# End units of both batches first, keys stored by batch, values of a phase in six shared tiles: a fused attention and gated projection kernel

## The chip, the cores and the metric

The kernel runs on one core of a Trainium2 chip. The metric is the device time of one execution in microseconds, lower is better.

## The reference

Block-sparse attention for 4 batches, 8 heads, 768 positions in 24 blocks of 32, head size 64. A query block attends to its own block and its two neighbours, to the first and the last block, and to three blocks drawn for it at run time; the first and the last query block attend to everything. Then a gated layer: a causal convolution of width 5 over the positions gives a gate, and the gated value projection is projected again.

```python
scores = scale * np.matmul(q, k.transpose(0, 1, 3, 2))
mask = np.abs(blk_i - blk_j) <= window
mask = mask | (blk_i == 0) | (blk_j == 0) | (blk_i == n_blocks - 1) | (blk_j == n_blocks - 1)
for qb in range(n_blocks):
    for kb in sampled_blocks[qb]:
        mask[qb * block:(qb + 1) * block, kb * block:(kb + 1) * block] = True
attn = softmax(np.where(mask, scores, -1e9))
x = np.matmul(attn, v)                      # heads side by side: (4, 768, 512)
gate_pre = sum over k of conv_w[k] * xp[:, k:k + S, :]
return (1.0 / (1.0 + np.exp(-gate_pre)) * (x @ w_val)) @ w_out
```

## The kernel before

Two phases of two batches each (`F`, `E`). The work of a phase is a list of parts: 22 pair parts (one inner query block i for both batches) and two end parts (query blocks 0 and 23 of one batch), which `GLOB_AT` puts at places 7 and 13 of phase 0. A pair part is one unit, an end part two, so there are 52 units.

A unit goes through four stages in successive steps of the main loop: `scores` (matmuls into PSUM, maximum on VectorE, exponential on ScalarE), `transposes` one step later (TensorE, evicted by ScalarE), `values` two steps later, `finish` three steps later (VectorE writes the rows, transposed, into `xT`). A pair unit scores 8 blocks held side by side in a ring of key tiles `kg`, filled by `copy_keys`: GpSimd copies blocks out of the tile `keys`, which holds all keys of the phase, by block and then by batch, and from block 19 on SP loads the drawn blocks from memory. Its values come as two operands: `va` (first and last block in the upper half, the pair's own two blocks in the lower, loaded by SP) and `vb` (neighbour and three drawn blocks, gathered by an indirect DMA on GpSimd with indices `idx`). An end unit scores against all 24 blocks in `keys` and takes its values from `vn`, one tile per batch in one buffer.

Three more jobs run beside the units. `decode_weights` turns 64-bit weights into two 32-bit parts on VectorE, `gates` and `split` prepare 384 rows of one batch for the layer on VectorE and ScalarE, `project` does its matmuls on TensorE. There are eight such row groups; the first needs all weights decoded and 12 query blocks finished. How many calls of them stand in each step is written out by hand in two strings of digits, two per step: `FILLS` (calls of `project`, 11 per row group) and `STEPS` (calls of decode, four per weight, or of a gate, 20 each; each group of them also advances a split). `WEIGHTS_AT`, `K_AT`, `KEY_PARTS` and `V_AT` say at which step or part a load is issued; all on SP's queue, in program order. Every engine's program order is fixed. At the start, 17 matmuls on a tile of ones keep TensorE busy (`WARM`), and VectorE computes the validity of the drawn blocks and the gather indices before the first unit.

Of the kernel before, what the change touches and what calls it, by code (L numbers as in the profile page):

```python
# [39 lines left out]
WARM = 17  # L40
# [5 lines left out]
    "41531212300155012103532311"  # L46
    "01035112303331022123021212"
    "00101201115004112130012510"
    "10100011122154101010100113"
    "4130"  # L50
)
STEPS = (
    "15212121013020010424122120"
    "21003221303420341233043241"
    "11132111152345310421322323"
    "14511004324143101000444354"
    "5525"
# [5 lines left out]
def attention_moe(ctx, tc, qb, kb, v, ve, sampled, w_val, conv_w, w_out, ident_in, slot_in, out):  # L63
# [11 lines left out]
    class InOrder:  # L75
# [23 lines left out]
    sp.dma_start(  # L99
        sb.rearrange("p i r w -> p (i r w)"),  # L100
        bass.AP(tensor=src.tensor, offset=src.offset, ap=[[0, 128], [1, NB * NR * 2]]),
    )
# [12 lines left out]
    act.activation(warm, warm, AF.Exp)  # L115
    sm = const.tile([1, NB * NR], I32, name="sm")
    dve.tensor_copy(sm, sb[0:1, :, :, 0].rearrange("p i r -> p (i r)"))
    sf = const.tile([128, NR, NB], F32, name="sf")
    dve.tensor_copy(sf, sb[:, :, :, 0].rearrange("p i r -> p r i"))

    base = const.tile([128, NB], F32, name="base")
    valid = const.tile([128, NB], F32, name="valid")
    off = slot[:, 2 * NB : 2 * NB + 1]
    dve.tensor_scalar(out=base[0:32, :], in0=slot[0:32, 0:NB], scalar1=off[0:32], scalar2=None, op0=ALU.add)
    dve.memset(valid, 1.0)
    dve.memset(valid[0:32, 1:2], 0.0)
    dve.memset(valid[0:32, NB - 2 : NB - 1], 0.0)
    vm = const.tile([128, NR, NB], F32, name="vm")  # L130
    tmp = const.tile([128, NR, NB], F32, name="tmp")
    dve.tensor_scalar(out=vm, in0=sf, scalar1=0.0, scalar2=None, op0=ALU.not_equal)
    dve.tensor_scalar(out=tmp, in0=sf, scalar1=float(NB - 1), scalar2=None, op0=ALU.not_equal)
    dve.tensor_tensor(out=vm, in0=vm, in1=tmp, op=ALU.mult)
    for r in range(NR):
        dve.tensor_tensor(out=tmp[:, r, :], in0=sf[:, r, :], in1=slot[:, NB : 2 * NB], op=ALU.subtract)
    dve.tensor_tensor(out=tmp, in0=tmp, in1=tmp, op=ALU.mult)
    dve.tensor_scalar(out=tmp, in0=tmp, scalar1=1.5, scalar2=None, op0=ALU.is_gt)
    dve.tensor_tensor(out=vm, in0=vm, in1=tmp, op=ALU.mult)
    for r in range(1, NR):  # L140
        for e in range(r):
            dve.tensor_tensor(out=tmp[:, 0, :], in0=sf[:, r, :], in1=sf[:, e, :], op=ALU.not_equal)
            dve.tensor_tensor(out=vm[:, r, :], in0=vm[:, r, :], in1=tmp[:, 0, :], op=ALU.mult)
    for r in range(NR):
        rows = slice(32 * (r + 1), 32 * (r + 2))
        dve.tensor_copy(valid[rows, :], vm[rows, r, :])
        dve.tensor_scalar(
            out=base[rows, :], in0=sf[rows, r, :], scalar1=float(BLK), scalar2=off[rows], op0=ALU.mult, op1=ALU.add
        )
    idx = const.tile([128, F, NB], I32, name="idx")  # L150
    def indices(f):

        row = const.tile([128, NB], F32, tag=f"row{f}", name="row")
        dve.tensor_scalar_add(row, base, float(f * S - F * S))
# [11 lines left out]
    waiting, copies, holding = [], [], [False]  # L166
# [84 lines left out]
    for f in range(F):  # L251
        ph = Phase()
        ph.f = f
        ph.xT, ph.vn = {}, {}
        ph.done, ph.queued, ph.read = set(), set(), [set() for _ in range(NT)]
        phases.append(ph)

    phase_of = [-1] * NB

    def load_all_keys():  # L260
        for f in range(F):
            for a, z in KEY_PARTS[f]:
                sp.dma_start(keys[:, a:z], kb[:, f, a:z])
                phase_of[a:z] = [f] * (z - a)
                yield

    def load_phase_values(ph):
        for e in range(E):
            vn = ph.vn[e] = const.tile([128, S // 128, H * DV], F32, tag="vn", name="vn")
            for c in range(3):  # L270
                r0 = ph.f * S + 256 * c
                sp.dma_start(
                    vn[:, 2 * c : 2 * c + 2, :],
                    v[r0 : r0 + 256, e * H * DV : (e + 1) * H * DV].rearrange("(c p) d -> p c d", p=128),
                )
# [9 lines left out]
    for ph in phases:  # L285
# [3 lines left out]
        for place, i in enumerate(order):  # L289
# [4 lines left out]
            if not pr.glob:  # L294
                pr.j, pr.p = (i - 1) % 2, (i - 1) // 2
                pr.kg = kg[pr.seq // 2 % 2]
# [6 lines left out]
    def block_numbers(pr, eng):  # L303
# [9 lines left out]
        for n, reg in zip(mine, regs):  # L313
            yield 1 + n, reg

    def one(block):
        return block.rearrange("p o e x -> p (o e x)")
# [5 lines left out]
    def load_keys(pr):  # L323
# [3 lines left out]
        if f and pr.i == 2:  # L327
            sp.dma_start(pr.kg[:, 0, 0:2], kb[:, f, 0 : NB : NB - 1])
        if not pr.glob:
            for place, reg in block_numbers(pr, SP):  # L330
                sp.dma_start(one(pr.kg[:, 1 + pr.j, place : place + 1]), one(kb[:, f, bass.ds(reg, 1)]))
# [546 lines left out]
```

## Time and profile before

| | us |
|---|---|
| median of 3 runs | 358.65 |
| lowest and highest | 357.97, 362.62 |
| the profiled execution's own time | 356.5 |
| its span, first to last instruction | 354.7 |
| TensorE busy in the span | 330.0 |
| VectorE busy | 273.8 |
| ScalarE busy | 229.5 |
| GpSimd busy | 96.6 |

The span is counted from the first instruction of the program; what lies around it is the difference to the time. Shares of busy time are means over stretches that have different limits, and TensorE's busy time is modelled, so the rows below are of stretches and of single instructions.

### The profile page before, as it was taken

The page shows a single profiled execution, that of the slowest core. Times are in us where ns is not written, and L with a number is a line of the kernel's source. Part 1 is how long each engine was busy: PE and PEld are TensorE (multiplying, and loading weights), DVE is VectorE, ACT ScalarE, POOL GpSimd, SP SyncE. Part 2 cuts the span into 40 slices and gives each one's busy share as a digit, 9 for nine tenths or more (in the row PEclk, how much of TensorE's full clock was granted, in tenths as well). Part 3 has the DMA queues.
Part 4 walks back from the last instruction along what each step waited for, and adds up shares of the span by engine and source line. Part 5 has one row for each costly group of instructions (what it writes and reads, how often), then busy time and mean ns, then how long its engine had stood idle before and what let it go on. Part 6 is the DMA issues. An engine that isn't in the chain of part 4 may idle for free.

```text
span 354.7 us, 15350 instructions
## 1 busy us (share of the span) xinstructions
PE 330.0 (93%) x6530; PEld 260.0 (73%) x6530; DVE 273.8 (77%) x665; ACT 229.5 (65%) x512; POOL 96.6 (27%) x146
## 2 busy tenths in 40 slices
PE   8589878887988999999999999999999999999995
PEld 7256656665655887797778777887778877988894
DVE  4277759978999899658988995659986489989640
ACT  2396657987888667656676674767667495565421
POOL 0776346536432032414331122221132010000000
PEclk9969989999999999999999999999999999999999
DMA  7998868876489997997698476636896022010202
GB/s 260 343 321 244 264 226 268 270 226 203 117 261 277 386 295 249 300 297 225 216 269 266 130 253 206 198 99 213 242 277 200 5 63 91 2 68 23 89 0 89
DMA packets 36707, 71.20 MB, mean 201 GB/s; under 512 B 4320, under 2 KB 21216, under 8 KB 36256
## 3 DMA queue, kind: packets, MB, share of 16 engines
q1 hardware_dynamic: 29728, 46.56, 41.5%
q0 software_dynamic: 6336, 23.43, 21.0%
q8 instruction: 51, 0.84, 1.0%
q10 hardware_dynamic: 576, 0.24, 0.2%
q14 instruction: 16, 0.13, 0.1%
HBM read 63.92 MB, written 6.29 MB: 198 GB/s over the span
## 4 chain that ended last, share of the span: by engine, by line
PE 59%; DVE 25%; ACT 8%; issue 3%; DMA 3%; SPq 0%; POOLq 0%; POOL 0%; ACTq 0%; DVEq 0%
PE op L81 13%; PE vp L81 12%; PE av L81 11%; PE pt L81 10%; PE sc L81 9%; DVE th L81 9%; DVE mx L81 6%; ACT pe L81 3%; DMA k<-in_k 3%; PE s L81 3%; ACT ptr L81 2%; DVE xl L81 2%; ACT th L81 2%; DVE wst L81 1%; DVE y L81 1%
## 5 line engine op out<-in xcount | busy, mean ns | idle before, releaser
L81 ACT ACTIVATE pe<-sc,mx 128x256 f32<-128x256 f32 x176 | 69.4, 478 | 42.1 <-DVE mx L81 42.0
L81 POOL DMA_INDIRECT vb<-in_v,idx x44 | 45.5, 1034 | 176.4 <-PE av L81 152.8
L81 DVE SCALAR_TENSOR_TENSOR th<-xT,cw,th 128x384 f32<-128x384 f32 x128 | 76.6, 625 | 4.6 <-ACT th L81 4.6
L81 DVE TENSOR_REDUCE mx<-sc 128x2 f32<-128x512 f32 x88 | 56.4, 681 | 30.7 <-PE sc L81 30.7
L81 ACT COPY ptr<-pt 128x512 f32<-128x512 f32 x112 | 63.7, 607 | 13.2 <-PE pt L81 11.6
L81 PE MATMUL sc<-kg,qc 64*32 64x256 f32 x1408 | 53.9, 393 | 9.1 <-ACT pe L81 3.3
L81 POOL COPY kg<-k 128x256 f32 (+1 forms) x97 | 50.6, 560 | 11.7 <-PE sc L81 10.8
L81 PE MATMUL op<-wo,yh 128*128 128x512 f32 x192 | 52.9, 397 | 0.1
L81 PE MATMUL pt<-ident,pe 128*128 128x128 f32 x352 | 52.5, 285 | 0.1
L81 PE MATMUL vp<-xh,wv 128*128 128x384 f32 x256 | 51.4, 342 | 0.0
L81 PEld LDWEIGHTS pt<-ident,pe 128*128 128x128 f32 x352 | 39.8, 143 | 6.8 <-issue 0.8
L81 PEld LDWEIGHTS vp<-xh,wv 128*128 128x128 f32 x256 | 44.1, 188 | 0.6 <-DVE y L81 0.4
L81 PEld LDWEIGHTS sc<-kg,qc 64*32 64x32 f32 x1408 | 22.9, 108 | 28.7 <-issue 12.8
L81 PEld LDWEIGHTS av<-va,ptr 128*32 128x32 f32 x1408 | 23.2, 110 | 25.3 <-ACT ptr L81 12.0
L81 PEld LDWEIGHTS op<-wo,yh 128*128 128x128 f32 x192 | 35.1, 188 | 7.2 <-ACT yh L81 0.5
L81 PE MATMUL av<-va,ptr 128*32 128x65 f32 x1408 | 32.3, 224 | 4.4 <-ACT ptr L81 2.0
L81 ACT CAST yh<-y 128x384 fp32r<-128x384 f32 x32 | 16.8, 524 | 22.8 <-DVE y L81 22.8
L81 PE MATMUL op<-wo,yl 128*128 128x512 f32 x96 | 30.8, 402 | 0.0
L81 PE MATMUL av<-vb,ptr 128*32 128x65 f32 x1408 | 28.9, 220 | 1.9 <-issue 1.9
L81 PE MATMUL vp<-xl,wv 128*128 128x384 f32 x128 | 27.4, 334 | 0.0
L81 DVE TENSOR_TENSOR yl<-y,yh 128x384 fp32r<-128x384 f32 x32 | 18.2, 568 | 10.4 <-ACT yh L81 10.1
L81 PEld LDWEIGHTS av<-vb,ptr 128*32 128x32 f32 x1408 | 23.8, 110 | 2.2 <-issue 2.0
(73 smaller groups left out, 389.6 us busy)
## 6 DMA issues: line engine op xcount, KB each, us to landing
kg<-in_k SPq DMA_DIRECT2D x78, 128.0 KB, 5.0
vn<-in_v SPq DMA_DIRECT2D x12, 520.0 KB, 6.3
qc<-in_q SPq DMA_DIRECT2D x48, 128.0 KB, 4.6
out<-ot SPq DMA_DIRECT2D x23, 256.0 KB, 2.4
va<-in_v SPq DMA_DIRECT2D x22, 260.0 KB, 5.9
k<-in_k SPq DMA_DIRECT2D x3, 1024.0 KB, 8.3
k<-in_k SPq DMA_DIRECT2D x6, 512.0 KB, 7.0
wst<-in_w_val SPq DMA_DIRECT2D x4, 512.0 KB, 8.4
```

Of the source, the lines that this page charges most:

```text
L81: made = getattr(self.eng, name)(*args, **kwargs)
```

## The change

The end parts of phase 0 go to places 0 and 0, so units 0 to 3 are end units, batch 0 first. `keys` is laid out by batch and then by block, and loaded per batch in thirds, batch 0 ahead of everything but the first query tile; the block numbers come behind it. End units score in four groups of matmuls (blocks 0 and 23; 1 to 6; 7 to 14; 15 to 22) in place of three. The values of a phase lie in six tiles of 128 rows for both batches, in memory with block 23 next to block 0, so that `ve` is no longer an input; in phase 0 a pair's `va` is one of these tiles or a tile filled by GpSimd copies of 64 rows, and in phase 1 every second pair's rows still come by a DMA. Validity and base rows move from VectorE to GpSimd, and the indices are computed in step 3. Of an end unit's three evictions in phase 0 the middle one moves from ScalarE to VectorE. Load places, warming matmuls and both strings of digits are other ones.

```diff
-GLOB_AT = ((7, 13), (12, 18))
-V_AT = ((6, 8, 10, 13, 13, 14), (0, 5, 12, 20, 23, 23))
-KEY_PARTS = (((16, 24), (0, 8), (8, 16)), ((0, 4), (4, 8), (8, 12), (12, 16), (16, 20), (20, 24)))
-K_AT = (0, 0, 0, 22, 23, 24, 24, 25, 25)
+GLOB_AT = ((0, 0), (12, 18))
+V_AT = ((0, 0, 1, 1, 1, 1, 2, 2, 3, 4, 4, 5), (0, 0, 3, 12, 12, 16))
+KEY_PARTS = (((0, 0, 8), (0, 8, 16), (0, 16, 24), (1, 0, 8), (1, 8, 16), (1, 16, 24)), tuple((E, a, a + 4) for a in range(0, NB, 4)))
+K_AT = (0, 0, 0, 1, 1, 1, 22, 24, 24, 24, 27, 29)
-WEIGHTS_AT = (0, 2, 6, 7, 8, 10, 15, 19)
+WEIGHTS_AT = (2, 6, 8, 9, 11, 12, 14, 19)
-WARM = 17
+VALUES_FROM = 4
+INDEX_AT = 3
+WARM = 13
+EVICTED = (4,)
 FILLS = (
+    "03551521524012114220200213"
+    "11120302053001132011022121"
+    "03100402104453112111312511"
+    "10100001111545201000000101"
+    "2154"
 STEPS = (
+    "35440005001114434131202031"
+    "01301003113322311155014114"
+    "55402320303154220043344354"
+    "23450102032554452123143312"
+    "4525"
...
+    def validity():
+        pool.tensor_scalar(out=base[NR * BLK :, :], in0=slot[NR * BLK :, 0:NB], scalar1=off[NR * BLK :], scalar2=None, op0=ALU.add)
+        pool.memset(valid, 1.0)
...
+        pool.tensor_scalar(out=vm, in0=sf, scalar1=0.0, scalar2=None, op0=ALU.is_gt)
+        pool.tensor_scalar(out=tmp, in0=sf, scalar1=float(NB - 1), scalar2=None, op0=ALU.is_lt)
+        pool.tensor_tensor(out=vm, in0=vm, in1=tmp, op=ALU.mult)
...
-    keys = const.tile([128, NB, E, HP * BLK], F32, name="k")
+    keys = const.tile([128, E, NB, HP * BLK], F32, name="k")
...
-        for e in range(E):
-            vn = ph.vn[e] = const.tile([128, S // 128, H * DV], F32, tag="vn", name="vn")
...
+        for e in range(E if ph.f == 0 else 1):
+            for c in range(S // 128):
+                if e == 0:
+                    ph.vn.append(const.tile([128, E, H * DV], F32, tag=f"vn{c}", name="vn"))
+                r0 = ph.f * S + 128 * c
+                some = slice(e, e + 1) if ph.f == 0 else slice(0, E)
+                sp.dma_start(ph.vn[c][:, some], v[r0 : r0 + 128, :].rearrange("p (e d) -> p e d", e=E)[:, some])
...
+        if pr is parts[0]:
+            load_numbers()
...
-            if first:
-                act.copy(kt[:, 0, 0:2], keys[:, 0 : NB : NB - 1])
-            (act.copy if first else pool.tensor_copy)(kt[:, 0, 2:4], keys[:, i0 : i0 + 2])
-            pool.tensor_copy(kt[:, 1:3, 0], keys[:, i0 - 1 : i0 + 3 : 3])
+            if pr.ph.f == 0 and i0 == 1:
+                pool.tensor_copy(kt[:, 0, 0:2], blocks(0, NB, NB - 1))
+            pool.tensor_copy(kt[:, 0, 2:4], blocks(i0, i0 + 2))
+            pool.tensor_copy(kt[:, 1:3, NR], blocks(i0 - 1, i0 + 3, 3))
...
-            if pr.p < 2 - (f == 0):
-                sp.dma_start(vt[0 : 2 * BLK].rearrange("p e d -> p (e d)"), ve[f])
-            sp.dma_start(vt[64:128].rearrange("p e d -> p (e d)"), v[r0 : r0 + 2 * BLK, :])
+            c, r0 = divmod(2 * BLK * (pr.p + 1), 128)
+            pr.va = va[pr.p % 2] if r0 == 0 or f else ph.vn[c]
+            ends = [] if pr.p == 0 or f == 0 and r0 == 0 and pr.p > 1 or f and pr.p > 2 else [ph.vn[0][0 : 2 * BLK]]
+            own = [ph.vn[c][0 : 2 * BLK]] if r0 == 0 else []
...
+            def copy_rows():
+                for rows in ends:
+                    pool.tensor_copy(pr.va[0 : 2 * BLK], rows)
+                for rows in own:
+                    pool.tensor_copy(pr.va[2 * BLK :], rows)
+            owns.append(copy_rows)
...
-            for k0 in range(3):
+            for dst, a, z, by in ((lo, 0, NB, NB - 1), (lo, 1, 7, 1), (lo, 7, 15, 1), (hi, 15, NB - 1, 1)):
...
-            act.copy(t, pt)
+            (dve.tensor_copy if un.pr.glob and un.pr.ph.f == 0 and len(un.PT) in EVICTED else act.copy)(t, pt)
...
-            indices(0)
-            more_keys()
-            more_values()
-            more_values()
-            until("copied", 1, copy_keys)
+            while more_keys():
+                pass
+            block_copies()
+            validity()
+        elif n < VALUES_FROM:
+            until("copied", 5, copy_keys)
+            while more_keys():
+                pass
...
+            if n == INDEX_AT:
+                indices(0)
...
+                run(owns)
...
-    nc = bacc.Bacc("TRN2", target_bir_lowering=False, num_devices=1)
+    nc = bacc.Bacc("TRN2", target_bir_lowering=False, num_devices=1, dynamic_dma_scratch_size=4096)
```

## Rows read from the trace of the kernel before

**Rows 1.** Chain of work that ended last: start, us, what.

```profile
2.61 10.49 DMA k<-in_k
14.38 1.20 PE sc L81 x32
...
115.80 4.17 PE vp L81 x24
...
342.51 8.25 PE op L81 x36
```

**Rows 2.** The same chain, single stages of units, without a wait inside.

```profile
28.31 1.05 PE av L81 x64
29.36 1.02 PE pt L81 x8
30.39 1.02 PE sc L81 x32
...
219.24 1.46 PE s L81 x48
...
226.37 1.50 PE av L81 x96
```

**Rows 3.** Busy time by stretch; columns: length, PE, PEld, DVE, ACT, POOL, clock, DMA.

```profile
15.56:56.80 41.24, 34.99 (x937) 23.46 (x938) 29.71 (x74) 29.71 (x68) 24.63 (x42) 0.88 0.86 272
56.80:110.90 54.10, 46.68 (x1396) 32.63 (x1393) 49.68 (x119) 44.45 (x104) 24.36 (x43) 1.00 0.74 226
115.60:297.00 181.40, 180.77 (x3711) 145.91 (x3710) 146.46 (x357) 123.68 (x277) 40.58 (x47) 1.00 0.70 217
297.00:354.70 57.70, 53.14 (x325) 46.99 (x323) 38.50 (x78) 24.87 (x51) 0.00 (x0) 1.00 0.12 46
```

**Rows 4.** Timeline of the head: warming matmuls, first key copies and what they waited for.

```profile
1.11 10.02 PE L81 MATMUL idle<-ones 128*128 128x256 f32 x34 [1.11 <-POOL ones L81]
10.41 1.14 ACT L81 COPY kg<-k 128x512 f32<-128x512 f32 x2 [4.79 <-DMA k<-in_k]
```

**Rows 5.** Timeline, VectorE: reductions of unit 0, of both end units, of the next.

```profile
15.56 1.29 DVE L81 TENSOR_REDUCE mx<-sc 128x2 f32<-128x512 f32 x2 [6.15 <-PE sc L81]
...
43.19 1.02 DVE L81 TENSOR_REDUCE mx<-s 128x1 f32<-128x512 f32 x2 [0.93 <-PE s L81]
...
50.26 1.02 DVE L81 TENSOR_REDUCE mx<-s 128x1 f32<-128x512 f32 x2 [2.54 <-PE s L81]
...
56.80 1.24 DVE L81 TENSOR_REDUCE mx<-sc 128x2 f32<-128x512 f32 x2
```

**Rows 6.** Groups by shape: count, busy us, mean ns of one, idle time before.

```profile
L81 DVE SCALAR_TENSOR_TENSOR th<-xT,cw,th 128x384 f32<-128x384 f32 x128 | 76.6, 625 | 4.6 <-ACT th L81 4.6
L81 DVE TENSOR_REDUCE mx<-sc 128x2 f32<-128x512 f32 x88 | 56.4, 681 | 30.7 <-PE sc L81 30.7
L81 POOL DMA_INDIRECT vb<-in_v,idx x44 | 45.5, 1034 | 176.4 <-PE av L81 152.8 <-DVE idx L81 8.6 <-issue 8.3
L81 POOL COPY kg<-k 128x256 f32 x54 | 21.8, 441 | 0.7 <-DMA k<-in_k 0.6
L81 DVE TENSOR_TENSOR x<-av,rs 128x256 f32<-128x256 f32 x48 | 19.9, 414 | 0.4
L81 DVE STREAM_TRANSPOSE xT<-x 128x256 f32<-128x256 f32 x44 | 18.9, 431 | 0.0
L81 DVE RECIPROCAL rs<-rs 128x4 f32<-128x4 f32 x48 | 7.7, 160 | 0.1
L81 DVE SCALAR_TENSOR_TENSOR wst<-wst 128x512 int32<-128x512 int32 x8 | 6.6, 827 | 0.1
```

**Rows 7.** Timeline: one decode instruction with and without GpSimd copies beside it.

```profile
25.45 1.39 DVE L81 SCALAR_TENSOR_TENSOR wst<-wst 128x512 int32<-128x512 int32 x1
25.53 1.55 POOL L81 COPY kg<-k 128x256 f32 x3
...
38.18 0.70 DVE L81 SCALAR_TENSOR_TENSOR wst<-wst 128x512 int32<-128x512 int32 x1
```

More of the change, by code (lines that the diff above doesn't have):

```diff
@@ L62, in attention_moe @@
 @with_exitstack
-def attention_moe(ctx, tc, qb, kb, v, ve, sampled, w_val, conv_w, w_out, ident_in, slot_in, out):
+def attention_moe(ctx, tc, qb, kb, v, sampled, w_val, conv_w, w_out, ident_in, slot_in, out):
     nc = tc.nc
@@ L137, in attention_moe @@
[L137 to L148, printed above, removed]
-        )
@@ L164, in attention_moe @@
     cw = const.tile([128, CH, KW], F32, name="cw")
-    waiting, copies, holding = [], [], [False]
+    waiting, copies, owns, holding = [], [], [], [False]
     def behind(*calls):
@@ L295, in attention_moe @@
                 pr.j, pr.p = (i - 1) % 2, (i - 1) // 2
+                pr.first = [x for x in parts if not x.glob][-1] if pr.j else pr
                 pr.kg = kg[pr.seq // 2 % 2]
@@ L313, in block_numbers @@
         for n, reg in zip(mine, regs):
-            yield 1 + n, reg
-    def one(block):
-        return block.rearrange("p o e x -> p (o e x)")
+            yield n, reg
     def load_queries(pr):
@@ L327, in load_keys @@
         if f and pr.i == 2:
-            sp.dma_start(pr.kg[:, 0, 0:2], kb[:, f, 0 : NB : NB - 1])
+            for n in range(2):
+                sp.dma_start(pr.kg[:, 0, n], kb[:, f, :, n * (NB - 1)])
         if not pr.glob:
             for place, reg in block_numbers(pr, SP):
-                sp.dma_start(one(pr.kg[:, 1 + pr.j, place : place + 1]), one(kb[:, f, bass.ds(reg, 1)]))
+                sp.dma_start(pr.kg[:, 1 + pr.j, place], kb[:, f, :, bass.ds(reg, 1)].rearrange("p e o x -> p e (o x)"))
         for _ in range(K_AT.count(parts.index(pr))):
             next(loading_keys)
+        if pr is parts[0]:
+            load_numbers()
         if pr is not parts[-1]:
@@ L337, in load_keys, with blocks @@
             next(loading_values[f])
+    def blocks(a, z, by=1):
+        return keys[:, :, a:z:by].rearrange("p e n x -> p n e x")
     def copy_keys(pr):
@@ L343, in copy_keys @@
         numbers = {eng: list(block_numbers(pr, eng)) for eng in (POOL, ACT)}
-        assert set(phase_of[i0 - 1 : i0 + 3] if pr.j == 0 else ()) <= {pr.ph.f}
-        assert not any(numbers.values()) or set(phase_of) == {pr.ph.f}
+        mine = {(f, e) for f in range(pr.ph.f + 1) for e in range(E)}
+        assert all(x == mine for x in (phase_of[i0 - 1 : i0 + 3] if pr.j == 0 else ()))
+        assert not any(numbers.values()) or all(x == mine for x in phase_of)
         if pr.j == 0:
-            first = pr.ph.f == 0 and i0 == 1
-            if first:
-                act.copy(kt[:, 0, 0:2], keys[:, 0 : NB : NB - 1])
-            (act.copy if first else pool.tensor_copy)(kt[:, 0, 2:4], keys[:, i0 : i0 + 2])
-            pool.tensor_copy(kt[:, 1:3, 0], keys[:, i0 - 1 : i0 + 3 : 3])
+            if pr.ph.f == 0 and i0 == 1:
+                pool.tensor_copy(kt[:, 0, 0:2], blocks(0, NB, NB - 1))
+            pool.tensor_copy(kt[:, 0, 2:4], blocks(i0, i0 + 2))
+            pool.tensor_copy(kt[:, 1:3, NR], blocks(i0 - 1, i0 + 3, 3))
         for place, reg in numbers[POOL]:
-            pool.tensor_copy(one(kt[:, 1 + pr.j, place : place + 1]), one(keys[:, bass.ds(reg, 1)]))
+            pool.tensor_copy(kt[:, 1 + pr.j, place], keys[:, :, bass.ds(reg, 1)].rearrange("p e o x -> p e (o x)"))
         def rest():
             for place, reg in numbers[ACT]:
-                act.copy(one(kt[:, 1 + pr.j, place : place + 1]), one(keys[:, bass.ds(reg, 1)]))
+                act.copy(kt[:, 1 + pr.j, place], keys[:, :, bass.ds(reg, 1)].rearrange("p e o x -> p e (o x)"))
             if pr.i == 3:
```

114 lines of the change are left out of this document (57 added, 57 removed).

## The prediction

> **What bounds the kernel now.** I read the chain of work that ended last first, then the busy time by stretch, then the instructions of the stretches that the chain points to. The chain begins with a DMA of keys that ends at 13.10 us, the first scores follow at 14.38, and from 115.80, the first matmul of a projection, to 350.76, the last, it is nearly all TensorE [rows 1]. So the kernel has three parts: a head without work for TensorE, a stretch with units alone, and from 115.80 a stretch in which projections fill every gap.
>
> That the last stretch is TensorE's own can be worked out without its busy share, which is modelled. A pair unit costs it 1.02 (scores) + 1.02 (transposes) + 1.05 (values) = 3.09 us, an end unit 1.46 + 1.5 x 1.02 + 1.50 = 4.49 [rows 2], a projection 2 x 4.17 + 8.25 = 16.59 [rows 1]. 44 pair units, 8 end units and 8 projections make 136.0 + 35.9 + 132.7 = 304.6 us. By 115.80 the scores of units 0 to 22, the values of 0 to 20 and the transposes of 0 to 20 and half of 21 are done: 73.1 us. The other 231.5 are done in the 238.9 us that are left, 3.9 of which come after the last matmul. TensorE's lost time is therefore nearly all ahead of 115.80: 42.7 us, of which 14.4 are the head and 28.3 lie between units.
>
> What makes the units slow there is VectorE. From the first reduction to that of unit 9 it is busy 29.71 of 41.24 us, from there to the reduction of unit 21 49.68 of 54.10, while TensorE has 3.09 us of work in a step of some 4.1 [rows 3]. It decodes the weights and makes the first gates in these steps. Later it has slack (146.46 of 181.40) and TensorE has none [rows 3].
>
> The time therefore follows from one number: when the first projection starts, and how many units are done by then. From the digits of STEPS, 36 decode calls, 20 calls for a gate and 6 for a split, I count that the first projection starts in step 22 before and in step 23 after. So after the change one more pair unit is done when it starts, and end = start + 238.9 - 3.1.
>
> **The change part by part.**
> *Head.* Before, the first scores need copies from two of three 1 MB pieces, and the second 1 MB has landed at 10.41 [rows 4], the third at 13.10 [rows 1]: 2.7 us per MB. After, unit 0 reads the keys of one batch straight from their tile, three pieces of 0.5 MB, with one query tile ahead. Counted back from 10.41 by half a MB, they land at about 9.0. The warming matmuls took 10.02 us for 34 records from 1.11 on [rows 4]; 13 in place of 17 of them end at about 8.8. Bounds for the first scores: 8.8 and 10.4; I take 9.0, so the first reduction is at 10.2 (before 15.56): 5.4 us earlier.
>
> *Four end units in a row.* A step between two end units can't be shorter than TensorE's 4.49. Before, the reductions of the two end units and of the unit behind them stand at 43.19, 50.26 and 56.80: steps of 7.1 and 6.5 us, with four decode calls in the second [rows 5]; after, steps 2 and 3 have no decode call. Bounds 4.5 and 6.8. I take 4.8, nearer to the lower end since VectorE has 2 x (1.02 + 0.16) of reductions and one eviction of 0.7 in such a step (its length from the reduction of as many elements, 0.681 [rows 6]) and waits for the rest of it. Unit 4 is reduced at 10.2 + 19.2 = 29.4; then two pair steps with an end unit's values or transposes in them (3.95 + 0.4) and three of 3.95, the mean from 15.56 to 43.19, seven steps [rows 5]: unit 9 at 49.9, against 56.80.
>
> *VectorE from unit 9 to the projection.* To the reduction of unit 21 it had 49.68 us. After, to that of unit 22: one more pair unit (2 x 0.681 + 0.414 + 0.431 + two small ones of 0.16 = +2.5); both end units have left this stretch (-2.0 in reductions); decode calls 22 in place of 16, at most 0.827 each (+5.0); gate calls 12 in place of 21, some 8 multiply-adds of 0.625 fewer (-5.0) [rows 6]. Sum +0.5. The four evictions moved to VectorE lie in the end steps, where it waits, and cost nothing; without that cover 2.8 us. Validity leaves VectorE at a time when it was idle: worth nothing.
>
> *GpSimd beside VectorE.* GpSimd gets some 7 copies of 64 x 1040 values in this stretch, in place of DMAs. No row has one: by elements it is four times the 256-element copy, at most 4 x 0.441 = 1.8 us [rows 6]; I take 1.3. A VectorE instruction of 0.70 us took 1.39 while three GpSimd copies ran for 1.55 [rows 7], so at most 0.45 us is lost per us of copying: 0 to 4.1, I take 2.0. [...] With the old idle time of 4.4 the stretch takes 49.7 + 0.5 + 2.0 + 4.4 = 56.6 us. Unit 22 is reduced at 106.5; the projection starts 4.9 later, as before (110.90 to 115.80): 111.4. Bounds for the idle time: 0, and 8.8 as twice the old.
>
> *Behind the start.* Gate calls that were done by then are owed later, 5.0 us of VectorE. Its slack of 35 us in that stretch [rows 3] hides that if it falls in the right steps; bounds 0 and 5, I take 1.0. End units have 32 score matmuls in place of 24 for the same 768 columns. 16 of their records are 64 columns wide; at the 0.0164 us that a 65-column record costs (1.05 / 64) [rows 2] that is 0.14 us a unit, 0.6 for the four units of the second phase. Bounds 0 and 2.
>
> *Hidden parts.* Validity on GpSimd is 27 instructions of at most 0.441 us each: up to 12 us from about 10, when the block numbers (now behind the keys on SP's queue) have landed. Behind them on GpSimd wait the key copies for unit 4, 4 us, ready by 26 at the latest, needed at 28. That cover is thin at its upper end; each us over it would be paid once. The index computation sits in step 3 on VectorE, and the first gather follows in step 4; its rows are needed at step 6, 8 us later. SP issues some 20 loads at the start; the first batch's values are behind 5.0 MB, at 2.7 us per MB about 18, and are needed in step 2, about 20. The removed value DMAs were late for nobody. On SP the reload of the first value tile waits for GpSimd's last copy out of it, and the second phase's key loads are queued behind; they are needed some three steps later.
>
> **The sum.** 111.4 + 238.9 - 3.1 + 1.0 + 0.6 = 348.8 us of span, 5.9 under 354.7. The profiled execution took 356.5 us, 1.8 more than its span, and the median of the runs is 358.65. Taking the saving from the median: 352.7. A measurement here can tell about 2%, 7.2 us, from no change.
>
> **The rivals.**
> *More than that.* If the end steps take 4.5 us and the idle 4.4 us of the second stretch vanish, because steps with pair units alone are more even, the start is at 105.8 and the time 347.1. For it: VectorE's load per step is evener. Against: decode calls crowd into steps 8 to 17.
> *The early start is lost again.* Weights arrive later (first decode of a weight in step 5, not 2), and 6 decode calls are moved into the stretch where VectorE is already 92% busy. If unit 22 comes no earlier than unit 21 did, only 3.1 - 1.6 are left: 357.1. The change would then have moved the wait from the keys to VectorE.
> *GpSimd becomes the bound, and it is slower than before.* For two units it makes two gathers of 1.034, six copies of 256 elements and two of 512 [rows 6]. At the 0.52 us a piece of 256 that it took beside VectorE [rows 7] this is 2.1 + 5.2, and a row copy of four pieces adds 2.1: 9.4 us, where two steps are 8.2. From unit 4 to 19 that is 0.6 us a unit, 9.6 in all: 362.3. At 0.44 it comes to 8.2 and just fits, so a contended copy decides. Against it: the copies for a unit are asked for two steps ahead, and the first nine units before, seven of them pairs, kept GpSimd busy for only about 60% of the time (24.63 of 41.24) [rows 3].
>
> **How the numbers follow.** Forecast 0.41 (352.7, its own range 348 to 357), more 0.26, lost again 0.19, GpSimd 0.14. Faster by over 2% (under 351.5) is the second case and a third of the forecast: 0.39. Slower by over 2% (over 365.8) is a third of the last: 0.05. The range leaves out half of the last case and the far end of the second: 345.5 to 361.
>
> **What would show it.** First scores near 9.0 and no idle TensorE before them; reductions of the end units 4.5 to 5.5 us apart; first projection matmul near 111 with the scores of unit 23 done; VectorE over 90% busy in the 50 us before; from there TensorE as full as before. Wrong if the first projection starts after 114, if key copies on GpSimd release scores again and again, or if VectorE's two-input instructions are longer throughout.

## The result and the profile after

The changed kernel takes 360.12 us (median of 20 runs, 356.69 to 362.65), the kernel before 358.78 in the same comparison (20 runs); the ratio is 1.0056 with a 95% interval of 1.0031 to 1.0081. The forecast was 352.7 and faster; 360.12 lies near the upper end of the whole range given, 345.5 to 361. Medians here are over all runs of a comparison and ratios over undisturbed runs alone, so the two can differ by a few tenths of a per cent. The profiled execution took 360.51 us with a span of 358.7 (before 356.5 and 354.7).

Busy time by stretch, kernel after, columns as in [rows 3]: first reduction to unit 9, unit 9 to the end of unit 22's reduction, the projections, the tail.

```profile
10.67:53.70 43.03, 36.19 (x1126) 26.46 (x1111) 30.14 (x78) 28.75 (x65) 30.69 (x65) 0.96 0.71 246
53.70:116.70 63.00, 49.62 (x1358) 34.95 (x1356) 60.02 (x127) 45.11 (x108) 46.44 (x66) 0.92 0.69 219
120.50:299.00 178.50, 176.01 (x3660) 142.30 (x3659) 147.43 (x352) 122.46 (x273) 47.72 (x54) 1.00 0.63 193
299.00:358.70 59.70, 56.10 (x337) 49.82 (x335) 40.04 (x81) 25.68 (x51) 0.00 (x0) 0.99 0.14 53
```

The first row shows what the head gave: 10.67 where [rows 5] had 15.56. The second shows where it went: VectorE (third pair of numbers) is busy 60.02 of 63.00 us, and GpSimd's 46.44 us are nearly twice the 24.36 of [rows 3]. TensorE's granted clock, 1.00 there before, is 0.92.

The chain of work that ended last, kernel after (start, us, what): the whole of it, then its pieces between 100 and 125 us.

```profile
1.10 8.45 PE idle L84 x26
13.16 2.91 PE s L84 x61
...
80.92 3.16 DVE wo L84
...
100.68 1.93 DVE th L84
...
120.96 3.39 DVE th L84 x2
...
346.74 8.38 PE op L84 x36
```

Before the projections it runs over VectorE, and the pieces that stick out are single decode and gate instructions of two to three us, where [rows 6] has 0.6 to 0.8. Their surroundings, timeline of the kernel after (start, us, engine, line, operation, tiles, count, and in brackets the idle time before and what ended it):

```profile
61.42 0.96 POOL L84 DMA_INDIRECT vb<-in_v,idx  x1 [0.52 <-PE av L84]
61.49 0.67 DVE L84 SCALAR_TENSOR_TENSOR wst<-wst 128x512 int32<-128x512 int32 x1
62.19 2.90 DVE L84 SCALAR_TENSOR_TENSOR words<-words,wst 128x512 int32<-128x512 int32 x1
62.38 1.06 POOL L84 COPY vn<-vn 64x1040 f32<-64x1040 f32 x1
63.38 2.65 POOL L84 COPY kg<-k 128x512 f32<-128x512 f32 x5
65.57 0.67 PE L84 MATMUL av<-va,ptr 128*32 128x65 f32 x32 [2.41 <-DVE x L84]
...
80.38 0.96 POOL L84 DMA_INDIRECT vb<-in_v,idx  x1 [1.28 <-PE av L84]
80.85 3.24 DVE L84 TENSOR_TENSOR wo<-words,wo 128x512 fp32r<-128x512 f32 x1
81.34 1.06 POOL L84 COPY vn<-vn 64x1040 f32<-64x1040 f32 x1
82.34 2.69 POOL L84 COPY kg<-k 128x512 f32<-128x512 f32 x5
84.89 1.09 PE L84 MATMUL av<-va,ptr 128*32 128x65 f32 x32 [2.77 <-DVE x L84]
86.79 1.78 PE L84 MATMUL pt<-ident,pe 128*128 128x128 f32 x8
90.58 1.09 PE L84 MATMUL pt<-ident,pe 128*128 128x128 f32 x8
```

The row copy (64 x 1040, new in this kernel) stands directly behind a gather and ahead of five key copies, so GpSimd copies for 3.7 us without a gap, and no gap lies between the gather and the first copy either. A VectorE instruction of 0.7 us that falls into that run lasts 2.9 or 3.2; both of these began while the gather still ran. Behind it on VectorE waits the small multiply that frees the values' PSUM tile, and TensorE idles 2.4 and 2.8 us for it (`<-DVE x`). After the second of these idle times the eight transposes take 1.78 us instead of 1.09. Busy time by short stretches there, the clock is the third number from the end:

```profile
74.00:78.00 4.00, 3.67 (x80) 3.20 (x88) 3.23 (x9) 2.48 (x7) 2.97 (x7) 0.57 0.18 58
84.80:88.50 3.70, 3.60 (x72) 3.29 (x73) 2.73 (x8) 2.07 (x5) 1.57 (x4) 0.54 0.02 4
104.00:109.00 5.00, 5.00 (x108) 3.26 (x112) 5.00 (x13) 2.90 (x8) 1.12 (x1) 0.66 1.03 338
```

Read in half microseconds, the granted clock is 0.50 from 75.0 to 78.0, from 85.3 to 87.8 and from 105.5 to 108.5. Groups by shape in the stretch from unit 9 to unit 22, kernel after (count, busy us, mean ns of one, idle before):

```profile
L84 DVE TENSOR_REDUCE mx<-sc 128x2 f32<-128x512 f32 x28 | 17.8, 673 | 0.9 <-PE sc L84 0.9
L84 DVE SCALAR_TENSOR_TENSOR th<-xT,cw,th 128x384 f32<-128x384 f32 x11 | 8.3, 771 | 0.0
L84 DVE SCALAR_TENSOR_TENSOR words<-words,wst 128x512 int32<-128x512 int32 x5 | 6.1, 1218 | 0.0
L84 DVE TENSOR_TENSOR x<-av,rs 128x256 f32<-128x256 f32 x13 | 5.3, 411 | 0.0
L84 DVE TENSOR_TENSOR wo<-words,wo 128x512 fp32r<-128x512 f32 x3 | 4.7, 1550 | 0.0
L84 DVE TENSOR_SCALAR words<-wst 128x512 f32<-128x512 f32 x6 | 3.5, 582 | 0.0
```

Work that reads PSUM is as short as in [rows 6] (mx 673 ns, x 411); decode and gates are longer, the decode ones up to twice (wo 1550 ns, where the kernel before has 785 from unit 9 to unit 21). Taking for each instruction the median of its kind without a copy beside it, I sum the excess: 9.9 us in this stretch, 3.2 in the same stretch before (unit 9 to unit 21). Below this is called the holding.

GpSimd's copies in the stretch by shape, three lines after the change and one before:

```profile
L84 POOL COPY kg<-k 128x256 f32 x31 | 15.8, 544 | 0.0
L84 POOL COPY va<-vn 64x1040 f32<-64x1040 f32 x4 | 4.3, 1076 | 0.2
L84 POOL COPY vn<-vn 64x1040 f32<-64x1040 f32 x3 | 3.2, 1062 | 0.0
...
L81 POOL COPY kg<-k 128x256 f32 x24 | 9.8, 447 | 0.0
```

The row copies are 7.5 of the 22.1 us that GpSimd has more. The rest comes from 11 more key copies, the short ones longer (544 ns for 447), and five more gathers, since the stretch now holds 14 pair units and no end unit, where it held 11 and two.

### The profile page after: what moved, and what is told of

Same layout as the page of the kernel before. It is cut to its first block, busy times and chain, and to the rows that moved or that the text cites. A ratio compares the mean times of both kernels' runs of the same rounds, so it can differ in the third digit from the quotient of the medians.

```text
span 358.7 us, 15589 instructions
## 1 busy us (share of the span) xinstructions
PE 330.8 (92%) x6650; PEld 263.6 (73%) x6650; DVE 281.9 (79%) x644; ACT 226.3 (63%) x505; POOL 126.8 (35%) x193
## 3 DMA queue, kind: packets, MB, share of 16 engines
q0 software_dynamic: 6336, 23.43, 20.5%
## 4 chain that ended last, share of the span: by engine, by line
PE 71%; DVE 19%; ACT 7%; issue 2%; POOL 0%; ACTq 0%; POOLq 0%; DVEq 0%
PE op L84 18%; PE vp L84 17%; PE av L84 12%; PE pt L84 10%; PE sc L84 8%; DVE mx L84 4%; DVE th L84 4%; PE s L84 4%; ACT ptr L84 2%; ACT pe L84 2%; PE idle L84 2%; DVE words L84 2%; DVE wst L84 2%; DVE xT L84 1%; DVE wo L84 1%
## 5 line engine op out<-in xcount | busy, mean ns | idle before, releaser
L84 DVE SCALAR_TENSOR_TENSOR th<-xT,cw,th 128x384 f32<-128x384 f32 x128 | 83.5, 681 | 1.5 <-ACT th L84 1.5
L84 ACT COPY ptr<-pt 128x512 f32<-128x512 f32 x108 | 61.4, 604 | 13.3 <-PE pt L84 12.7
L84 POOL COPY kg<-k 128x256 f32 (+1 forms) x99 | 55.6, 598 | 8.9 <-PE sc L84 8.2
L84 PE MATMUL sc<-kg,qc 64*32 64x256 f32 x1408 | 53.7, 387 | 2.7 <-ACT pe L84 2.6
L84 PEld LDWEIGHTS av<-vn,ptr 128*32 128x32 f32 x1216 | 19.1, 110 | 17.8 <-issue 7.7
L84 PEld LDWEIGHTS av<-va,ptr 128*32 128x32 f32 x960 | 15.8, 111 | 21.8 <-issue 9.8
L84 PE MATMUL av<-vn,ptr 128*32 128x65 f32 x1216 | 23.4, 223 | 7.7 <-issue 3.1
L84 PE MATMUL av<-va,ptr 128*32 128x65 f32 x960 | 21.6, 227 | 8.1 <-DVE x L84 5.2
```

What stands on the lines that cost most here:

```text
L84: made = getattr(self.eng, name)(*args, **kwargs)
```

## The experiments

Theory 1: the row copies on GpSimd hold VectorE's instructions, and that eats the head's gain. Theory 2: decode and gates stand too late. Other rivals: the head's gain never reached the end; four end units in a row are dear; validity costs GpSimd. Each kernel was compared with the kernel before on the same chip. The chips differ between experiments (medians of the kernel before from 357.43 to 358.78 us), so two changed kernels are better compared by their ratios than by their medians.

**1. Does the head reach the end?** 26 warming matmuls in place of 13, so that the first scores start late.

```
-WARM = 13
+WARM = 26
```

> The changed kernel with 26 warming matmuls in place of 13, which hold TensorE until about 14.6 us, so that the first scores start where they did before the change. Theory 1 (the early start reaches the end of the kernel and is spent elsewhere): 5 us slower than the changed kernel, 364 to 366. Rival (the early start is hidden behind something that sets the pace up to unit 9, such as key copies, weights or gathers that come no earlier): 360 to 362, with unit 9 reduced within 2 us of where it was.

Measured 366.12 us, ratio 1.022 [1.0179, 1.0261]; the first reduction at 16.2, 5.5 us later, and the time 6.0 us longer. The gain of the head is whole at the end; something else takes as much.

**2. Row copies elsewhere, or twice.** `copy_rows` on ScalarE, as loads from memory on SP's queue, and each copy made twice.

In `rows_dma` (end rows; the own rows likewise):

```
-            def copy_rows():
-                for rows in ends:
-                    pool.tensor_copy(pr.va[0 : 2 * BLK], rows)
...
+            for _ in ends:
+                sp.dma_start(pr.va[0 : 2 * BLK].rearrange("p e d -> p (e d)"), v[f * S : f * S + 2 * BLK, :])
```

In `rows_act` and in `rows_twice` (the line for own rows likewise):

```
-                    pool.tensor_copy(pr.va[0 : 2 * BLK], rows)
+                    act.copy(pr.va[0 : 2 * BLK], rows)
```

```
                     pool.tensor_copy(pr.va[0 : 2 * BLK], rows)
+                    pool.tensor_copy(pr.va[0 : 2 * BLK], rows)
```

> The changed kernel, with the 64-row value copies made by DMAs on SP's queue in place of GpSimd. Theory 1 (GpSimd's row copies join its key copies into runs that hold VectorE's two-input instructions; 6.8 us more of that ahead of the first projection than before the change): no VectorE instruction ahead of the first projection longer than 1.6 us, first projection near 114, time 353 to 355, some 6 us under the changed kernel's 360.1. Theory 2 (the decoding is only asked for later, and VectorE's own work fills the stretch): first projection at 119 to 121, time 359 to 361.

> The changed kernel, with the 64-row copies on ScalarE in place of GpSimd. Theory 1: ScalarE is busy 45 of 63 us in the stretch and takes 7 copies of 1.07 us without setting the pace: time 354 to 357, long VectorE instructions gone as with DMAs. Theory 2: no gain, 360 to 362, since ScalarE has more to do and VectorE as much as before.

> The changed kernel, with every 64-row copy made twice on GpSimd. Theory 1: a second 1.06 us in each run of copies holds VectorE's instruction that much longer wherever one is held: single instructions of 3 to 4.5 us, first projection 4 to 8 us later, time 364 to 368. Theory 2: GpSimd is busy 46 of 63 us and has room for 7 more: time 360 to 362.

Measured: by DMA 359.79, 1.0026 [0.9982, 1.007]; on ScalarE 359.96, 1.0074 [1.0036, 1.0112]; twice 366.34, 1.0263 [1.0209, 1.0316]. Doubling costs 6.2 us in the median, as Theory 1 says. Its profiled execution (362.73) does not show the way that Theory 1 expects, though: the first projection starts at 120.58 where it started at 120.50, the longest VectorE instruction ahead of it lasts 2.3 us (3 to 4.5 were expected), and the 2.2 us that this execution is longer lie behind that start. Moving the copies gains nothing clear of the intervals. With them on ScalarE the holding from unit 9 to unit 22 fell from 9.9 to 7.1, while the weight loads of the values waited 19.6 us for ScalarE's evictions up to the projection (9.3 after). Each new place had a price of its own, so these three runs don't give that of the copies.

**3. Decode earlier.** Weights loaded and decoded from the first steps on.

```
-WEIGHTS_AT = (2, 6, 8, 9, 11, 12, 14, 19)
+WEIGHTS_AT = (0, 1, 2, 3, 7, 8, 10, 12)
-    "35440005001114434131202031"
-    "01301003113322311155014114"
+    "35440011111212121111111111"
+    "11111111112222312222014114"
```

> The changed kernel, with weights loaded at steps 0, 1, 2, 3, 7, 8, 10, 12 in place of 2, 6, 8, 9, 11, 12, 14, 19 and two or three decode calls in every step from 3 to 16; the projections stand in the same steps. Theory 1: the sum of VectorE's work is as before and the row copies still hold it; only the decode calls that now come ahead of the first row copies are saved: time 357 to 359. Theory 2: VectorE's idle 13 us ahead of unit 9 are used, the first projection starts 5 to 7 us earlier: time 353 to 355.

Measured 360.28, 1.0078 [1.0038, 1.0118]. VectorE's idle time up to unit 9 fell from 12.9 to 8.9 us, but unit 9 came at 57.0 in place of 53.7. The work that was put there met copies, too: the holding up to unit 9 rose from some 1.5 to 4.9 us (one decode instruction lasted 2.77), and VectorE waited 2.9 us for a weight's DMA. Neither theory's time came out. So this order of the decode calls gains nothing, but what an earlier decode clear of copies would give is not shown.

**4. Key copies by DMA.** The drawn key blocks come from memory from block 5 on: in the changed kernel, in the kernel before, and together with the rows as in `rows_dma`.

```
-LAST_COPIED = 18
+LAST_COPIED = 4
```

> The changed kernel, with the drawn key blocks of units from block 5 on loaded by SP's DMAs from memory in place of GpSimd copies, as the second phase does. Theory 1 (runs of GpSimd copies hold VectorE's two-input instructions, and the row copies only lengthen such runs): the runs are cut to one row copy and two key copies, stretching ahead of unit 22 falls from 11.5 us to 5 to 7, time 355 to 358. Theory 2 (the chain of scores, maximum, exponential and transposes sets the step, and VectorE's stretching is covered): 359 to 361. If loads on SP's queue are late instead, score matmuls wait for DMAs and it is slower, 362 or more.

> The kernel before the change, with the same edit: drawn key blocks from block 5 on by SP's DMAs. Theory 1: only 5.8 us of stretching stands there, so the gain is half of that in the changed kernel, 1 to 3 us: 356 to 358. Theory 2: no difference, 358 to 360.

> The changed kernel, with both the drawn key blocks from block 5 on and the 64-row value copies made by DMAs. Theory 1: GpSimd is left with gathers and two 512-element copies per pair, stretching ahead of unit 22 at 3 us or less, first projection near 113, time 352 to 355. Theory 2: first projection at 119 or later, 359 to 361.

Measured 362.04 (1.0107 [1.0073, 1.0141]), 368.46 (1.0277 [1.0229, 1.0324]) and 368.37 (1.0256 [1.0205, 1.0307]). The holding from unit 9 to unit 22 fell, as Theory 1 says, from 9.9 to some 6.4 us in `kg_dma` and 3.5 in `kg_rows_dma`, and in the kernel before from 3.2 to some 1.3, but all three became slower. Waits of TensorE between 15 and 115 us that end in "issue" (us in total, times, longest; the groups over 1.5 us), in this order: after, `kg_dma`, `kg_rows_dma`, before, `kg_dma_before`.

```profile
PE av L84 <- issue: 2.5, 3, 1.3
```

```profile
PE av L84 <- issue: 5.3, 5, 1.6
PE pt L84 <- issue: 2.8, 2, 1.7
PE sc L84 <- issue: 2.6, 2, 2.1
```

```profile
PE av L84 <- issue: 13.9, 10, 4.9
PE sc L84 <- issue: 1.9, 1, 1.9
```

```profile
PE av L81 <- issue: 3.5, 3, 1.9
PE sc L81 <- issue: 2.5, 2, 1.6
```

```profile
PE av L81 <- issue: 11.6, 6, 4.3
PE sc L81 <- issue: 2.4, 2, 2.2
```

"issue" is time in which nothing that the profile shows was waited for. One of them in the timeline of `kg_rows_dma`, in the middle of a group of 32 equal matmuls:

```profile
74.50 0.81 PE L84 MATMUL av<-vb,ptr 128*32 128x65 f32 x18 [4.91 <-issue]
```

The DMA engines' mean busy share from 15 to 115 us is 0.68 after, 0.84 in `kg_dma` and 0.92 in `kg_rows_dma`; 0.80 before and 0.88 in `kg_dma_before`. In these five, more DMA traffic and more such waits go together within each kernel. The share alone does not decide, though: the waits sum to 6.0 us at 0.80 in the kernel before and to 10.3 at 0.76 in `ends_dma` (experiment 7). That TensorE waits there for its instructions is my reading, not shown.

**5. Row copies left out, nothing in their place.** `rows_none` leaves out 15 of 18 row copies (first edit); `copies_none` also the drawn key copies from block 5 on (both edits); `copies_none_before` those alone in the kernel before (second edit).

```
-            owns.append(copy_rows)
+            if (f, pr.p) in ((0, 1), (1, 2)):
+                owns.append(copy_rows)
...
-        for place, reg in numbers[POOL]:
+        for place, reg in numbers[POOL] if pr.i < 5 else ():
```

> The changed kernel with 15 of its 18 row copies of 64 x 1040 left out (the two of pair 1 and one at the start of the second phase stay, so that each tile is written once): the values of some pairs are those of other rows, so the output is another one; nothing takes the place of the copies, neither a DMA nor ScalarE. Theory 1 (a VectorE instruction with two SBUF inputs waits for a run of copies on GpSimd, and the row copies lengthen the runs): VectorE's stretching up to unit 22 falls from 11 us to 5 to 7, the first projection starts some 4 us earlier, at about 116, and the median is 354 to 356.5, ratio to the kernel before 0.988 to 0.995. Rival (VectorE's own work and the order of the steps set the start of the projection, the stretching falls into its idle time): the first projection stays within 1 us of 120.5 and the median at 359 to 361.

> As rows_none, and the copies of the drawn key blocks from block 5 on left out as well (42 of 256 elements): those scores are of older blocks, so the output is another one. GpSimd has hardly any copies left beside the block's own and its neighbours'. Theory 1: stretching under 3 us up to unit 22, the first projection at 110 to 114, median 346 to 352. Rival: first projection at 118 or later, median over 356.

> The kernel before with the copies of the drawn key blocks from block 5 on left out (42 of 256 elements; the output is another one): the control for copies_none. Theory 1: its stretching falls from 5.8 us to under 2, but in the stretches where units with the end blocks and VectorE's idle time leave room, so the first projection moves by 1 to 3 us and the median is 354 to 357.5. Rival (drawn-block copies themselves release the scores late, so that they are on the path in both kernels): the gain is the same as in copies_none within 1.5 us.

Measured: `rows_none` 354.28, 0.9907 [0.987, 0.9944]; `copies_none` 351.39, 0.9848 [0.9811, 0.9884]; `copies_none_before` 357.54, 1.0007 [0.997, 1.0045]. Stretch from unit 9 to the end of unit 22's reduction in `rows_none`:

```profile
52.90:111.50 58.60, 47.81 (x1381) 32.97 (x1370) 54.93 (x126) 44.99 (x108) 38.29 (x58) 1.00 0.73 233
```

It takes 58.6 us in place of 63.0; the holding fell from 9.9 to 4.5, the clock is 1.00, the projection starts at 115.3 in place of 120.5. The decode instruction that lasted 2.90 at 62.19 in the changed kernel, and GpSimd beside it, in the timeline of `rows_none`:

```profile
62.14 1.35 POOL L84 DMA_INDIRECT vb<-in_v,idx  x1 [1.01 <-PE av L84]
62.70 0.69 DVE L84 SCALAR_TENSOR_TENSOR words<-words,wst 128x512 int32<-128x512 int32 x1
...
63.49 2.19 POOL L84 COPY kg<-k 128x512 f32<-128x512 f32 x5
```

Here it was through before the key copies began, beside the gather alone, so this line shows its length without copies and not a shorter hold.

Theory 1 holds: the row copies cost the changed kernel some 5.8 us in the medians (360.12 to 354.28) and 1.5%, or 5.3 us, in the ratios, as much as the head gained. Part of it goes with the clock. Over the 20 runs of the changed kernel a straight line through times and mean granted clocks falls by 1.8 us per 0.01; the mean clock is 0.986 in these runs and 0.998 in those of `rows_none`, so an estimated 2 of the 5.8 us go with TensorE's lower clock, whatever brings that about. The median of `copies_none` lies in Theory 1's range; its profiled execution, 4.6 us longer than the median, starts the projection at 116.2, past the 110 to 114 expected.

The control shows why the same kind of holding cost the old kernel nothing that can be measured: without the drawn key copies its holding up to the projection fell from some 5.8 to 1.7, VectorE's idle time rose from 16.0 to 19.1, and the projection came 0.2 us earlier. Unit 9 came 4.5 us earlier, but unit 15 at 79.9 in both. So there the holding lay in slack, while taking it out of the changed kernel brought the projection 5.2 us earlier.

**6. End units apart, validity on VectorE.** `split_ends` puts the second end part of phase 0 at place 6 (`GLOB_AT` (0, 6)); there it reads value tiles into which end rows have already been copied, so its output is another one. `validity_dve` gives the 27 validity instructions back to VectorE.

```
-GLOB_AT = ((0, 0), (12, 18))
+GLOB_AT = ((0, 6), (12, 18))
-VALUES_FROM = 4
-INDEX_AT = 3
+VALUES_FROM = 2
+INDEX_AT = 1
...
-        pool.tensor_scalar(out=vm, in0=sf, scalar1=0.0, scalar2=None, op0=ALU.is_gt)
+        dve.tensor_scalar(out=vm, in0=sf, scalar1=0.0, scalar2=None, op0=ALU.is_gt)
```

> The changed kernel with the second end part of the first phase moved from place 0 to place 6 (units 0, 1 and 8, 9 are end units), and values and indices two steps earlier; everything else as it is. Theory that four end units in a row cost: the forecast had their steps at 4.8 us, they took 4.5 to 6.5, so unit 9 or 10 would come 1 to 3 us earlier and the median would be 356.5 to 359. Rival (an end unit costs its step wherever it stands): median 359.5 to 362.

> The changed kernel with the validity of the drawn blocks back on VectorE (27 small instructions at the start), all else as it is. Theory (hidden in both places): VectorE is idle between the first reductions of the end units, so the median stays at 359 to 361.5 and the first four reductions come at most 1 us later. Rival (on VectorE they stand between the block numbers at 9.8 us and the first reduction): the first reduction 3 to 4 us later, of which the end keeps them, 362 to 364.

Measured 365.93, 1.0267 [1.0227, 1.0308], and 363.99, 1.0224 [1.0167, 1.028]. Neither theory of the first had a time over 362. Steps from an end to a pair unit and back took 6.8 to 8.5 us there (units 2, 3, 9 and 10), against 4.5 to 6.5 for the end units in a row; the digits of `STEPS` were those for the other order, so part of it may be theirs. For validity the rival is right. Timeline of `validity_dve`, the last of the block numbers' copies, the last validity instruction, the first reduction, and TensorE's first scores:

```profile
8.61 1.60 PE L84 MATMUL s<-k,qc 64*32 64x64 f32 x66
...
9.84 0.27 DVE L84 CAST sf<-sb 128x72 f32<-128x72 int32 x1
...
14.44 0.22 DVE L84 TENSOR_SCALAR base<-sf,slot 32x24 f32<-32x24 f32 x1
14.69 1.02 DVE L84 TENSOR_REDUCE mx<-s 128x1 f32<-128x512 f32 x2
```

The scores are there at 10.2 and wait for VectorE until 14.69. Without validity on GpSimd four of the head's five us are gone (in the times 3.9 us by the medians, 6.0 by the ratios).

**7. Which copies, and a version that beats both.** Only five copies of end rows are moved, to ScalarE, VectorE or SP's queue. They stand directly ahead of five key copies, or of two once the drawn blocks come from memory. The edit of `ends_act`; the others have VectorE's copy or a load in the same place:

```
-                    pool.tensor_copy(pr.va[0 : 2 * BLK], rows)
+                    (act.copy if f == 0 and pr.p > 1 else pool.tensor_copy)(pr.va[0 : 2 * BLK], rows)
```

> The changed kernel with five of its 18 row copies, those that put the end rows into a value tile (each stands directly ahead of five key copies on GpSimd), on ScalarE, at the same place of the program. Theory A (a VectorE instruction is held for the whole run, so the length of the run sets the price): the holds of 2.9, 3.2 and 2.0 us fall to 1 to 2, the stretching between units 9 and 22 from 9.9 to about 6, and the median is 355.5 to 357.5. Theory B (the sum of copying sets the price): 5/18 of the 5 to 6 us, so 358 to 359.5. Rival C (five copies of 1.06 us on ScalarE delay its evictions as all 18 did): 359.5 to 361.

> As ends_act, with the five copies on VectorE itself. A copy of 64 x 1040 takes it an estimated 0.6 to 1.1 us, three of them between units 9 and 22: 2 to 3.3 us more work there, some 4 less of stretching. Theory A: median 356.5 to 359. Theory B: 359.5 to 362, since VectorE is the bound there and gets the whole of the work.

> As ends_act, with the five copies as loads of 64 rows from memory on SP's queue. Theory A with little DMA traffic added (1.3 MB where all rows by DMA were 4.8): median 355.5 to 358 and TensorE's waits for instructions ahead of the first projection under 5 us. Rival (each added load costs TensorE as much as the copy cost VectorE): 359 to 361, with these waits over 6 us.

Measured 355.72 (0.9983 [0.9948, 1.0019]), 357.29 (1.0006 [0.9971, 1.0041]) and 356.33 (0.9984 [0.9946, 1.0022]). Against `rows_none` that is 4.4, 2.8 and 3.8 of 5.8 us in the medians, and in the ratios 0.73, 0.50 and 0.72 of 1.49%. The medians favour Theory A, the ratios stand between it and B. B's share was reckoned too low, too: of the seven row copies between units 9 and 22 three are among the five, and 3/7 of 1.49% is 0.64%. So run length and sum are not told apart by these times; that one instruction is held through several copies is shown by the rows alone. Single rows show that the length of the run is not all: in `kg_dma`, with two key copies behind a row copy, instructions still lasted 2.65 and 2.42 us (at 83.70 and 102.44), and in `ends_act_own_dma` below one lasted 2.71 (at 78.41) beside a gather and five key copies, without a row copy. `ends_dma` kept Theory A's time but not its sign: TensorE's waits ending in "issue" were 10.3 us, where under 5 were expected. On VectorE a copy took 0.68 us, and even there it cost no more than on GpSimd. Stretch from unit 9 to the end of unit 22's reduction in `ends_act`:

```profile
52.30:112.30 60.00, 47.94 (x1361) 32.33 (x1359) 57.27 (x126) 47.53 (x111) 42.41 (x63) 1.00 0.71 227
```

The holding is 7.4 there (Theory A expected about 6), 2.5 less than after, and the stretch 3.0 shorter, with the clock at 1.00. On top of `ends_act` two more, `ends_act_own_dma` and `ends_act_copied`:

```
+            if f == 0 and own and pr.p > 1:
+                own.clear()
+                sp.dma_start(
+                    pr.va[2 * BLK :].rearrange("p e d -> p (e d)"),
+                    v[2 * BLK * (pr.p + 1) : 2 * BLK * (pr.p + 2), :],
+                )
```

```
-COPIED = (POOL, POOL, POOL)
+COPIED = (POOL, POOL, ACT)
```

> ends_act, and the copies of a pair's own rows in the first phase (from the second such pair on, four of them, three between units 9 and 22) as loads of 64 rows from memory on SP's queue, issued where the pair's gather is issued. If the remaining row copies are what is left of the loss: stretching between units 9 and 22 falls from 7.4 to about 5, the median to 353.5 to 355.5. If loads cost TensorE what copies cost VectorE: 355 to 357.5, with more of TensorE's waits for instructions (2.3 us ahead of the first projection in ends_act) in their place.

> ends_act, and the third drawn key block of every pair unit of the first phase up to block 18 copied by ScalarE in place of GpSimd. Runs of key copies get shorter by one (5 to 4, 3 to 2). If runs of key copies are what is left of the loss: stretching between units 9 and 22 falls from 7.4 to 4 or 5 and the median to 353 to 355. If ScalarE's evictions pay for it (some 14 copies of about 0.4 us, 5.6 us of work beside 50 of 64 us): 356 to 360.

Measured 356.75 (0.9964 [0.9927, 1.0001]) and 355.46 (0.9947 [0.9911, 0.9983]). The last beats the kernel before by half a per cent and the changed one by some 4.7 us (3.9 by the ratios). Both medians miss the range of their first theory, by 1.3 and 0.5 us, so what is left was not found in own rows or in one key copy. The first lies in the range of its second theory, but without the sign that this theory named: TensorE's waits ending in "issue" were 1.9 us, against 2.3 in `ends_act`. In `ends_act_copied` the holding is 6.0 and ScalarE is busy 50.90 of 58.50 us of the stretch, against 45.11 of 63.00.

## Why the prediction was wrong

- **"The time follows from one number: when the first projection starts."** Right. From there to the last matmul it took 234.6 us (forecast 238.9 - 3.9 - 3.1 + 1.6 = 233.5, before 235.0). The owed gates and the longer end units of the second phase were sized well enough; nearly all that was missed lies ahead of the projection, which came at 120.5 and not at 111.4.
- **Head, 5.4 us.** Right: first scores 9.48, first reduction 10.67, 4.9 earlier, and it reaches the end whole (experiment 1).
- **"Validity leaves VectorE at a time when it was idle: worth nothing."** Wrong in its reason. It was idle for the old head; in the new one validity would stand between block numbers and first reduction, and moving it is worth four us or more (experiment 6). The sum was not hurt, since the early head was booked in full.
- **End units at 4.8 us, unit 9 at 49.9.** Mis-sized by 3.8, inside its bounds: the steps were 4.5, 4.9, 5.2 and 6.5, the second unit's scores took 2.91 us at a low clock (0.53 from 13.0 to 16.1 us; 1.46 us in [rows 2]), the pair steps behind them took 21.9 us for a forecast of 20.5.
- **VectorE's own work, +0.5 us.** Mis-sized: without holding it is 60.0 - 9.9 = 50.1 us after and some 49.7 - 3.2 = 46.5 before, so +3.6. I took 6 decode instructions more and some 8 multiply-adds fewer; the windows have 29 for 21 and 11 for 16. By their lengths without a copy beside them the eight decode instructions more cost some 5 us, as I had taken for six; five multiply-adds fewer gave back 3 and not 5, and the units' own instructions and the splits added the rest.
- **"I take 2.0" for GpSimd beside VectorE, at most 0.45 us lost per us of copying.** This is the step that failed. That the middle of 0 to 4.1 would hold was my estimate; no run shows it. The holding rose by 6.7 us, over the upper bound of 4.1; 5.4 us of the holding vanish with the row copies, and the stretch becomes 4.4 us shorter (experiment 5). The stretch took 63.0 us for a forecast of 56.6: 4.7 more for holding, 3.1 more for own work, 1.4 less of idle time. The rate came from one instruction in [rows 7], whose three copies were 1.55 us long; with a row copy ahead of five key copies the run is 3.7 us and the loss is 2.2 and 2.6 for one instruction, 0.6 to 0.7 per us of copying. The term also left out the key copies and gathers that the pair units in place of end units bring along; without row copies the holding is still 4.5, against 3.2 before. The copy's own length, 1.06 us, was even below the 1.3 I took.
- **Rivals.** "The early start is lost again in VectorE" (357.1) is what happened in outline: unit 22 came at 115.4, unit 21 at 109.6 before. That the decode calls it named are the cause is not shown: moving them early gained nothing, but they then met other copies (experiment 3). "GpSimd becomes the bound" gave the nearest time, 362.3, by a mechanism that did not occur: it was busy 46.4 of 63.0 us, and TensorE waited 0.3 us in all for key copies up to unit 22.
- Together: 0.5 + 1.9 + 1.4 to unit 9, then some 4.4 from row copies and 0.9 from the rest make the 9.1 us by which the projection was late. Without row copies the kernel takes 354.28, 1.6 from the forecast, but that nearness is partly luck: its projection starts 3.9 us later than forecast and its span is 352.4 for 348.8. The forecast took the saving in the span from a median that lay 2.15 us above the profiled execution. Two of its own signs of being wrong came true: a projection after 114, and longer two-input instructions.

Open: how much of the row copies' price is the holding itself and how much the lower clock of that stretch (0.92, against 1.00 in `rows_none` and `ends_act`, where the holding is less, too; the 2 us above are a correlation over runs, not an experiment), whether the length of a run or the sum of copying sets the price, whether the gather ahead of a run takes part in a hold, and what TensorE waits for in "issue".

## What to carry to other kernels

Before moving work to an idle GpSimd, look in the trace at how long its copies run without a gap and which VectorE instructions fall into that run; an instruction can be held for several copies (2.9 and 3.2 us for 0.7 here), and that was paid where VectorE was the bound (the projection came 5.2 us earlier in `rows_none`), not where it had slack (0.2 us in `copies_none_before`). A head that was hidden behind a load must be read again when the load gets earlier: what stood beside the wait now stands in the path. When moving a cost between engines or queues only trades it, leave the work out once, with nothing in its place, to learn what it costs.

## What the runs showed of the hardware

- A VectorE instruction with two SBUF inputs that met gapless copies on GpSimd lasted 2.9 and 3.2 us in the changed kernel (0.69 for the first beside a gather alone, in `rows_none`). The first began at 62.19, ahead of the row copy (62.38) but inside the gather in front of it (61.42 to 62.38), and ended at 65.09, 1.7 us into the key copies (63.38). So it lasted over the whole row copy and part of the key copies, though it began ahead of both; what decides when it is through is not shown. A `TENSOR_SCALAR` with one SBUF input was held too (582 ns in the mean, 469 in `rows_none`), reductions out of PSUM were not (673 and 673).
- TensorE stood still for 4.91 us in the middle of 32 equal matmuls in `kg_rows_dma`, with nothing that the profile shows; the sum of the waits shown between 15 and 115 us was 2.5 us at a DMA share of 0.68 (after) and 15.8 at 0.92 (`kg_rows_dma`), but 6.0 at 0.80 in the kernel before and 10.3 at 0.76 in `ends_dma`.
- The granted clock was 0.54 to 0.66 for three stretches of 3.7 to 5 us in the changed kernel, and its mean from unit 9 to unit 22 was 0.92 there and 1.00 in `rows_none` and `ends_act`; eight transposes took 1.78 us in the stretch at 0.54, against 1.09.
